# Retention and mixture of experts in one kernel: first expert half tiles beside the gate of the last batch

## The chip, the cores and the metric

One core of one Trainium2 chip. The metric is device time in microseconds of one launch. Before the change the median of three runs is 260.36 us (260.19 to 264.4).

## The reference

Two layers, one after the other. The first is a retention recurrence with a decay per head, over 4 batches, 8 heads, 768 steps and 64 columns. The second sends each of the 3072 rows of its output, 512 wide, through at most one of 8 experts.

```python
# q, k, v: (4, 8, 768, 64) float32
gamma = 1 - 2.0 ** (-5 - arange(H))
for t in range(S):
    state = gamma * state + einsum('bhd,bhe->bhde', k[:, :, t], v[:, :, t])
    y[:, :, t] = einsum('bhd,bhde->bhe', q[:, :, t], state) / sqrt(D)
x = y.transpose(0, 2, 1, 3).reshape(B * S, H * D)          # (3072, 512)

active = x @ w_skip > 0                                    # other rows are passed through
e_idx  = argmax(x @ w_gate, axis=1)                        # 8 experts
gate_w = softmax(x @ w_gate)[e_idx]
out = x;  out[row] += gate_w[row] * (relu(x[row] @ w1[e]) @ w2[e])   # active rows, w1: 512x1024, w2: 1024x512
```

Counted from the reference on the drawn inputs, 1510 rows are active, per expert 191, 133, 229, 179, 211, 187, 160 and 220. Of batches 0 to 2 alone these are 157, 98, 164, 126, 164, 132, 114 and 163.

## The kernel before, in words

**Attention units.** The loop at L471 runs over NU = 16 units `i`, a pair of heads of one batch each (batch `i // 4`). A unit scales the rows of later units on POOL (`scale_rows`, L91), turns rows on PE (`rows_t`, L231), computes states (`kv_states`, L243), scores (`scores`, L275, whose mask multiply `ATm` at L295 is on DVE) and values (`values`, L300, copied out as `xT` by DVE at L321 and ACT at L323). `rows_x` (L326) turns the result back into rows `xall` and in the same matmul makes partial logits `Lp`, copied out by ACT at L340 and L341. `store_x` (L343) writes a batch to `out` by a DMA on ACT's queue.

**Gate.** Each batch's gate is a chain of small steps: `gate_a` (logits, largest, active; DVE), `gate_exp` (ACT), `gate_count` (matmuls that count rows before each row; PE), `gate_pos`, `gate_sum`, `gate_b`, `gate_c` (DVE), `one_hots` (six one-hot matrices of a row's position among 256 slots, L433, DVE), `table` (twelve matmuls, L441, that sum row numbers and weights into a table of slots) and `table_add`. `Rsum` carries the counts over from batch to batch. For batches 0 to 2 the steps stand at fixed places in the units that follow the batch (L493 to L530), all six one-hots of a batch at one place. The last batch's steps stand behind the loop (L538 to L545). `slots` (L554) then turns the table into row indices `si` and weights `g` for both halves of the 256 slots.

**Experts.** An expert has a tile of CAP = 256 slots in NST = 2 parts of 128. `gather` (L579) fetches a part's rows from `out` by an indirect DMA on POOL's queue, six buffers for three experts ahead. `x_tr` (L591) casts them to bf16 on DVE (L595), turns them on PE (L599) and copies them on DVE (L600). `layer1` (L602) has 32 matmuls of 256 columns with four ReLU copies on ACT (L613). `layer2` (L616) has 16 matmuls of 512 columns (L620), a multiply-add with the gathered rows on DVE (L625) and a scatter by indirect DMA (L628). In PE's order the next expert's `x_tr` stands between `layer1` and `layer2`. The number of further passes, for an expert with more than 256 rows, is counted at L640 to L654 and loaded into a register of each engine; the loop at L669 runs that often.

**Weights.** The matrices are cast to bf16 by DMAs on POOL's queue: 28 quarter matrices (`load_piece`) in units 3 to 15 by the counts of `EARLY` (L456), each in the last two units behind a tiny POOL multiply that waits for a named tile, and 9 whole matrices (`load_whole`, L202) in the expert stage: two behind the gathers of expert 1, two behind those of expert 2, and two after each of the first experts until none is left. A drain of POOL stands before the first gather (L569), and one after expert 5 (L665). Instructions of an engine run in the order of the code.

Of the kernel before, what the change touches and what calls it, by code (L numbers as in the profile page):

```python
# [18 lines left out]
def kernel(  # L19
# [38 lines left out]
    NGA = 3  # L58
    NPASS = (N + CAP - 1) // CAP - 1
# [4 lines left out]
    poolC = ctx.enter_context(tc.tile_pool(name="constp", bufs=1))  # L64
    poolW = ctx.enter_context(tc.tile_pool(name="wpool", bufs=1))
# [96 lines left out]
    xrows = [poolC.tile([128, DM], FP32, name=f"xrows{t}") for t in range(NGA * NST)]  # L162
# [180 lines left out]
    def store_x(b, g):  # L343
        A_.dma_start(
            out=out[b * S : (b + 1) * S, :].rearrange("(g p r) d -> p g (r d)", p=128, r=R)[:, g, :],
            in_=xall[b][:, g * R : (g + 1) * R, :].rearrange("p r d -> p (r d)"),
        )
# [4 lines left out]
    def gtile(name, shape, dt=FP32):  # L352
        gt[name] = pool.tile(shape, dt, tag=name, bufs=1, name=name)
        return gt[name]
# [25 lines left out]
    def gate_count(b):  # L380
        ha = gt["ha"]
        cp = psum.tile([128, NCH, E], FP32, tag="T", bufs=2, name="cps")
# [24 lines left out]

    def gate_b(b):
# [28 lines left out]
    def table(js, oh, ps, tag, bufs):  # L437
        tp = ps.tile([128, NST, NV * E], FP32, tag=tag, bufs=bufs, name="tabps")
# [8 lines left out]
    def table_add(tp):  # L447
        t = Tsb[:, :].rearrange("p (s n) -> p s n", s=NST)
        V_.tensor_tensor(t, t, tp[:, :, :], ALU.add)

# [16 lines left out]

    for m in range(3):
        rows_t(0, m)
    kv_states(0)  # L470
    for i in range(NU):  # L471
        b, p = divmod(i - 5, NP)
# [7 lines left out]
        if i >= NP and i % NP == 1:  # L480
            store_x(i // NP - 1, G - 1)
        scores(i, 0)
        scale_rows(i + 2, 0, G_)
# [9 lines left out]
        if b >= 0 and p == 1:  # L493
            gate_count(b)
            gate_pos(b)
        if b >= 0 and p == NP - 1:
            table_add(table(batch_js(b), oh, psum, "T", 2))
# [5 lines left out]
        if b >= 0:  # L503

            if p == 0:
                gate_a(b)
            elif p == 1:
                gate_sum(b)
                gate_b(b)
            elif p == 2:  # L510
                gate_c(b)
                oh = one_hots(batch_js(b), pool)
# [5 lines left out]
        rows_x(i - 1, 1)  # L518
        if not late:
# [3 lines left out]
        if i and i % NP == 0:  # L523
            for g in range(G - 1):
                store_x(i // NP - 1, g)
# [3 lines left out]
        if b >= 0 and p == 0:  # L529
            gate_exp(b)  # L530
# [18 lines left out]

    poolX = ctx.enter_context(tc.tile_pool(name="wlate", bufs=1, reuse_waits="tile"))  # L550
    poolE = ctx.enter_context(tc.tile_pool(name="esb", bufs=2, reuse_waits="tile"))
    psE = ctx.enter_context(tc.tile_pool(name="eps", bufs=2, space=bass.MemoryType.PSUM, reuse_waits="tile"))

    def slots():  # L554

        T = Tsb[:, :].rearrange("p (s a e) -> p s a e", s=NST, a=NV)
        sh = [128, NST, E]
        tid = poolE.tile(sh, FP32, tag="tid", bufs=1, name="tid")
        V_.scalar_tensor_tensor(out=tid[:, :, :], in0=T[:, :, 0, :], scalar=256.0, in1=T[:, :, 1, :], op0=ALU.mult, op1=ALU.add)
        emp = poolE.tile(sh, FP32, tag="emp", bufs=1, name="emp")  # L560
        V_.tensor_scalar(emp[:, :, :], T[:, :, 1, :], 0.0, BIG, ALU.is_equal, ALU.mult)
        si = poolE.tile(sh, I32, tag="si", bufs=1, name="si")
        V_.scalar_tensor_tensor(out=si[:, :, :], in0=tid[:, :, :], scalar=-1.0, in1=emp[:, :, :], op0=ALU.add, op1=ALU.add)
        g = poolE.tile(sh, FP32, tag="g", bufs=1, name="g")
        V_.tensor_tensor(g[:, :, :], T[:, :, 2, :], T[:, :, 3, :], ALU.add)  # L565
        V_.tensor_tensor(g[:, :, :], g[:, :, :], T[:, :, 4, :], ALU.add)
        return si, g

    G_.drain()  # L569
    si, g = slots()  # L570
    xg, xgT = {}, {}

    gathers, scatters = [], []

    def free(ins, others):
        for o in others:
            tc.declare_no_dep(ins, o.ins, reason="the slots of a pass name distinct rows, empty ones none")

    def gather(e, si, first=False):  # L579
        for st in range(NST):  # L580
            t = xrows[(e % NGA) * NST + st]
            ga = G_.indirect_dma_start(  # L582
                out=t[:, :], out_offset=None, in_=out[:, :],
                in_offset=bass.IndirectOffsetOnAxis(ap=si[:, st, e : e + 1], axis=0), bounds_check=N - 1, oob_is_err=False,
            )
            xg[e, st] = t
            if first:
                free(ga.ins, scatters)
                gathers.append(ga)

# [119 lines left out]
```

## Time and profile before

| what | value |
|---|---|
| median of 3 runs | 260.36 us (260.19 to 264.4) |
| profiled execution | 261.43 us |
| its span, first to last instruction | 259.4 us |
| mean granted TensorE clock | 0.922 of full |
| busy: PE, DVE, ACT, POOL | 204.2, 120.5, 85.0, 104.8 us |
| DMA moved, mean rate | 48.72 MB, 188 GB/s |

The span is measured inside the execution; the 2.0 us between it and the execution's own time are around it. In a timeline row the bracket at the end names the idle time of the engine before the row and what ended it.

### The profile page before, as it was taken

Reading aid. Unit: us, or ns where it says so; the run is one execution under the profiler, and the core shown is the slowest. Engines: PE = TensorE matmul, PEld = TensorE weight load, DVE = VectorE, ACT = ScalarE, POOL = GpSimd, SP = SyncE. Lnnn points to the kernel's source line nnn. Section 1 sums busy time; section 2 is a strip of 40 time slices with the busy share of each in tenths; the row PEclk is TensorE's granted clock in tenths of the full one; section 3 lists DMA queues with packets and bytes.
Section 4 is the critical chain, followed back from the end, with each engine's and each line's share of the span. In section 5 each row is a group of like instructions: output and inputs, shape, how many; then the busy total and the mean of one; then the engine's idle time right before and its main releaser. Section 6 shows DMA issues by size and latency. Waiting matters only on the chain.

```text
span 259.4 us, 7927 instructions
## 1 busy us (share of the span) xinstructions
PE 204.2 (79%) x3405; PEld 163.9 (63%) x3405; DVE 120.5 (46%) x348; ACT 85.0 (33%) x192; POOL 104.8 (40%) x129
## 2 busy tenths in 40 slices
PE   2999989987897897995999942189837993988960
PEld 1778878876776786884888731177533662467730
DVE  6344445565677575676565658213402331134220
ACT  5244537433442542541445330032130312033110
POOL 1448466552641642642304310844425463143330
PEclk9999999999999997997999996589995998599995
DMA  6999997999688599467575984599999999241110
GB/s 186 300 241 292 283 268 171 270 311 205 173 204 207 195 246 262 132 111 121 165 163 75 145 160 195 121 197 247 215 260 205 268 238 263 89 139 59 40 56 34
DMA packets 48375, 48.72 MB, mean 188 GB/s; under 512 B 3684, under 2 KB 40548, under 8 KB 47184
## 3 DMA queue, kind: packets, MB, share of 16 engines
q0 software_dynamic: 7888, 22.97, 43.2%
q1 hardware_dynamic: 38720, 18.90, 26.5%
q10 hardware_dynamic: 1728, 6.29, 6.3%
q8 instruction: 29, 0.48, 0.7%
q14 instruction: 10, 0.08, 0.1%
HBM read 56.64 MB, written 10.49 MB: 259 GB/s over the span
## 4 chain that ended last, share of the span: by engine, by line
PE 46%; issue 17%; DMA 15%; DVE 10%; POOL 7%; ACT 1%; POOLq 1%; SPq 0%; ACTq 0%; DVEq 0%
PE tps L240 10%; PE tps L335 9%; PE atps L289 9%; DMA w1b<-in_moe_w_dram 8%; PE yps L313 7%; PE kvps L252 5%; DMA out_dram<-yo,si 5%; PE yps L269 5%; DVE oh L433 4%; POOL xrows L582 3%; POOL out_dram L628 3%; DVE ATm L295 2%; DMA xrows<-out_dram,si 1%; DMA kw<-in_k_dram 1%; PE tabps L441 1%
## 5 line engine op out<-in xcount | busy, mean ns | idle before, releaser
L295 DVE TENSOR_TENSOR ATm<-atps,maskc 128x384 f32<-128x384 f32 x64 | 32.8, 553 | 30.3 <-PE atps L289 29.4
L101 POOL TENSOR_TENSOR qs<-qw,tq 128x768 f32<-128x768 f32 x15 | 22.5, 1501 | 54.1 <-issue 46.8
L613 ACT ACTIVATE hT<-hps 128x512 bf16<-128x512 f32 x32 | 19.1, 597 | 72.9 <-PE hps L609 72.6
L241 ACT COPY QKT<-tps 128x512 f32<-128x512 f32 x48 | 28.0, 586 | 44.3 <-PE tps L240 43.5
L289 PE MATMUL atps<-QKT 64*64 64x128 f32 x768 | 36.7, 278 | 5.8 <-issue 5.0
L335 PE MATMUL tps<-IW,xT 128*128 128x137 f32 x192 | 30.6, 298 | 5.7 <-DVE xT L321 4.8
L628 POOL DMA_INDIRECT out_dram<-yo,si x16 | 16.2, 1014 | 46.1 <-DVE yo L625 34.7
L620 PE MATMUL yps<-w2b,hT 128*128 128x512 bf16 x128 | 33.8, 424 | 0.0
L289 PEld LDWEIGHTS atps<-QKT 64*64 64x64 f32 x768 | 28.7, 138 | 5.9 <-issue 4.4
L609 PE MATMUL hps<-xgT,w1b 128*128 128x256 bf16 x256 | 30.7, 279 | 0.5 <-DVE xgT L600 0.5
L609 PEld LDWEIGHTS <-w1b 128*128 128x128 bf16 x256 | 29.4, 145 | 2.6 <-issue 0.7
L335 PEld LDWEIGHTS tps<-IW,xT 128*128 128x128 f32 x192 | 25.9, 199 | 7.9 <-issue 4.0
L313 PE MATMUL yps<-ATm,vn 64*64 64x128 f32 x768 | 26.3, 272 | 2.8 <-issue 2.6
L101 POOL TENSOR_TENSOR ks<-kw,tk 128x768 f32<-128x768 f32 x15 | 22.4, 1495 | 13.5 <-DMA kw<-in_k_dram 10.1
L323 ACT COPY xT<-yps 64x384 f32<-64x384 f32 x32 | 15.2, 474 | 28.5 <-PE yps L313 27.7
L582 POOL DMA_INDIRECT xrows<-out_dram,si x16 | 16.9, 1053 | 18.4 <-DVE g L565 11.6
L625 DVE SCALAR_TENSOR_TENSOR yo<-yps,g,xrows 128x512 f32<-128x512 f32 x16 | 12.0, 751 | 26.3 <-PE yps L620 26.3
L620 PEld LDWEIGHTS <-hT 128*128 128x128 bf16 x128 | 13.6, 108 | 16.8 <-issue 6.3
L313 PEld LDWEIGHTS yps<-ATm,vn 64*64 64x64 f32 x768 | 21.8, 133 | 3.8 <-issue 2.9
L599 PE MATMUL xtp<-identb,xb 128*128 128x128 bf16 x64 | 7.7, 254 | 20.2 <-DVE xb L595 14.3
L240 PE MATMUL tps<-ident,ks 128*128 128x128 f32 x96 | 18.4, 306 | 4.9 <-DVE ks L101 4.9
L269 PE MATMUL yps<-QKT,St 64*64 64x128 f32 x320 | 20.8, 291 | 0.0
(101 smaller groups left out, 232.2 us busy)
## 6 DMA issues: line engine op xcount, KB each, us to landing
vn<-in_v_dram SPq DMA_DIRECT2D x16, 384.0 KB, 5.7
out_dram<-xall ACTq DMA_DIRECT2D x12, 512.0 KB, 4.6
kw<-in_k_dram SPq DMA_DIRECT2D x15, 384.0 KB, 7.0
qw<-in_q_dram SPq DMA_DIRECT2D x15, 384.0 KB, 7.7
w2b<-in_moe_w_dram POOLq DMA_DIRECT2D x5, 1024.0 KB
w1b<-in_moe_w_dram POOLq DMA_DIRECT2D x16, 256.0 KB
w1b<-in_moe_w_dram POOLq DMA_DIRECT2D x4, 1024.0 KB
w2b<-in_moe_w_dram POOLq DMA_DIRECT2D x12, 256.0 KB
```

What stands on the lines that cost most here:

```text
L101: eng.tensor_tensor(o[:, :, h, :], rows[:, :, h, :], sc[:, :, h, :], ALU.mult)
L240: PE.transpose(out=ps[:, j * 128 : (j + 1) * 128], in_=(ks, qs)[w][i][:, s_, :, :].rearrange("p h d -> p (h d)"), identity=ident[:, :])
L241: A_.copy(out=QKT[i][:, 4 * m : 4 * m + 4, :], in_=ps[:, :].rearrange("p (j t) -> p j t", j=4))
L269: PE.matmul(out=Y[i, c][o : o + 64, g, :], lhsT=St[i][t : t + 64, ch - 1, :], rhs=QKT[i][t : t + 64, NCH + R * g : NCH + R * g + R, 64 * c ...
L289: PE.matmul(out=ps[h][cp, j, :], lhsT=QKT[i][hp, a * SPB + j, cp], rhs=QKT[i][hp, NCH + R * g : NCH + R * g + R, cp], start=True, stop=True,)
L295: V_.tensor_tensor(out=ATm[i, a][:, t, :, :], in0=ps[t][:, :, :], in1=maskc[:, a * SPB : (a + 1) * SPB, :, :].rearrange("p s r t -> p s (r ...
L313: PE.matmul(out=Y[i, c][o : o + 64, g, :], lhsT=vn[i][cp, h * G + g, r * D : (r + 1) * D], rhs=ATm[i, a][cp, h, j, :], start=False, stop=l ...
L335: PE.matmul(out=ps[:, j * XW : (j + 1) * XW], lhsT=xT[i][:, a * (NCH // 2) + j, :], rhs=IW[:, p, :], start=True, stop=True, skip_group_che ...
L582: ga = G_.indirect_dma_start(out=t[:, :], out_offset=None, in_=out[:, :], in_offset=bass.IndirectOffsetOnAxis(ap=si[:, st, e : e + 1], axi ...
L609: PE.matmul(out=ps[:, f, :], lhsT=w1b[e][:, db, :].rearrange("p (c a) -> p a c", a=NFB)[:, fb, :], rhs=xgT[e][:, db, :], start=(db == 0), ...
L620: PE.matmul(out=ps[:, :], lhsT=hT[:, fb, st * 128 : (st + 1) * 128], rhs=w2b[e][:, fb, :], start=(fb == 0), stop=(fb == NFB - 1),)
L628: sc = G_.indirect_dma_start(out=out[:, :], out_offset=bass.IndirectOffsetOnAxis(ap=si[:, st, e : e + 1], axis=0), in_=yo[:, :], in_offset ...
```

## The change

Rows of batches 0 to 2 and of the last batch now get slots apart. A new step `gate_fill` raises each expert's count to at least 128 before the last batch is counted, so that its rows get slots from 128 on, and the first part of each tile is final once batch 2's table is added. `slots` works on a range of parts. The work of the experts becomes a list of tasks: the first parts of experts 0, 1 and 2, then their second parts, then experts 3 to 7 whole. `layer1` takes a tile of 128 or 256 columns, with one PSUM tile of 512 columns for four or two blocks.

Batch 2's gate moves forward by about a unit: its count to the end of unit 13, its one-hots to the end of unit 14, its table, the first slots and the filler to the middle of unit 15, and the first parts of experts 0 to 2 are gathered in unit 15. The one-hots of batches 0 and 1 are made in twos at three places over two units, and their table follows a unit later. The last batch's steps are laid among the first two tasks. The first three tiles are cast and moved by ACT. The last batch is stored through SP's queue. Row buffers become eight. Whole matrices, gathers and scatters follow a written plan by task, and POOL's first drain becomes a tiny multiply that waits for the last rows.

```diff
-    NPASS = (N + CAP - 1) // CAP - 1
+    NPASS = (N + 128 + CAP - 1) // CAP - 1
+    FIRST = 3
+    NROW = 8
...
+    def gate_fill(ps, tag, bufs):
+        cn = ps.tile([128, E], FP32, tag=tag, bufs=bufs, name="cnps")
+        PE.matmul(out=cn[:, :], lhsT=onesb[:, :], rhs=Rsum[:, :], start=True, stop=True)
+        fl = gtile("fl", [128, E])
+        V_.tensor_scalar(fl[:, :], cn[:, :], -1.0, 128.0, ALU.mult, ALU.add)
+        V_.tensor_scalar(fl[:, :], fl[:, :], 0.0, ident[:, 0:1], ALU.max, ALU.mult)
+        V_.tensor_tensor(Rsum[:, :], Rsum[:, :], fl[:, :], ALU.add)
...
+    def rows_of(st, first):
+        return (out[0:NOLD, :], NOLD) if first and st == 0 else (out[:, :], N)
...
+    for b in range(B - 1):
+        i, T = NP * b + NP + 1, (psum, "T", 2)
+        at(i, "b", (gate_a, b))
+        at(i, "end", (gate_exp, b))
+        if b < B - 2:
+            at(i + 1, "mid", (gate_count, b, *T), (gate_pos, b))
+            at(i + 1, "b", (gate_sum, b), (gate_b, b))
+            at(i + 2, "b", (gate_c, b), (one_hots_of, b, 2))
+            at(i + 3, "a", (one_hots_of, b, 2))
+            at(i + 3, "b", (one_hots_of, b, 2))
+            at(i + 4, "mid", (table_of, b, *T))
+        else:
+            at(i, "end", (gate_count, b, *T), (gate_pos, b))
+            at(i + 1, "a", (gate_sum, b), (gate_b, b))
+            at(i + 1, "b", (gate_c, b), (one_hots_of, b, NCH))
+            at(i + 2, "mid", (table_of, b, *T), (slots, slice(0, 1), "0"), (gate_fill, *T))
...
+        if i == NU - 1:
+            for e in range(FIRST):
+                gather(e, 0)
...
     values(NU - 1)
-    rows_x(NU - 1, 0)
-    table_add(table(batch_js(B - 2), oh, psum, "T", 2))
-    rows_x(NU - 1, 1)
     b = B - 1
+    for a in range(2):
+        rows_x(NU - 1, a)
     for g in range(G):
-        store_x(b, g)
+        store_x(b, g, nc.sync)
+    G_.tensor_tensor(junk[:, :], xall[b][0:1, NCH - 1, DM - 1 : DM], xall[b][0:1, NCH - 1, DM - 1 : DM], ALU.mult)
     gate_a(b)
...
+    def layer1(e, xgT):
+        n = xgT.shape[2]
...
+        m = 512 // n
+        for f2 in range(NFB // m):
+            ps = psE.tile([128, m, n], FP32, tag="hps", bufs=2, name="hps")
...
+    tasks = [(e, [0]) for e in range(FIRST)] + [(e, rest) for e in range(FIRST) if rest]
+    tasks += [(e, list(range(NST))) for e in range(FIRST, E)]
+    plan = {
+        None: "W", 0: "s0", 1: "gB W s1", 2: "s2 g3 W g4", 3: "s3 W", 4: "s4 g5 W", 5: "s5 W g6", 6: "s6 W g7", 7: "s7 W W",
+    }
...
+    give(None)
+    xgT = x_tr(*tasks[0], A_.copy, A_.copy)
+    gate_exp(b)
+    for k, (e, sts) in enumerate(tasks):
+        hT = layer1(e, xgT)
+        if k == 0:
+            gate_count(b, psE, "cnt", 1)
+            gate_b(b)
+            gate_pos(b)
+            one_hots_of(b, NCH)
+            gate_c(b)
+        if k == 1:
+            table_of(b, psE, "cnt", 1)
+            slots(slice(1, NST), "1")
+            gate_sum(b)
+        if k == FIRST:
+            n_more = passes()
+        if k + 1 < len(tasks):
+            early = k + 1 < FIRST
+            xgT = x_tr(*tasks[k + 1], A_.copy if early else V_.tensor_copy, A_.copy if early else V_.tensor_copy)
+        yos += layer2(e, sts, hT)
+        give(k)
+        if k == len(tasks) - 3:
+            G_.drain()
```

In the plan W is one whole matrix, g3 the gathers of expert 3, gB the gathers of the second parts of experts 0 to 2, and s the scatters of the tasks done so far. `passes` holds the count of L640 to L654 unchanged.

## Rows read from the trace of the kernel before

**Rows 1.** Busy time by stretch: columns are us, PE, PEld, DVE, ACT, POOL, PEclk, DMA share, GB/s

```profile
154.56:168.60 14.04, 3.12 (x28) 2.04 (x29) 8.37 (x42) 0.24 (x1) 5.87 (x7) 0.61 0.54 169
...
168.60:190.60 22.00, 20.21 (x144) 15.26 (x143) 6.08 (x12) 6.57 (x11) 9.12 (x11) 0.94 1.00 220
...
226.50:250.85 24.35, 22.56 (x162) 16.32 (x160) 7.54 (x14) 7.17 (x12) 7.73 (x8) 1.00 0.19 67
```

**Rows 2.** Timeline of the hole: start, us, engine, line, out<-in, count, idle before

```profile
154.37 0.19 ACT L341 COPY Lp<-tps 128x27 f32<-128x27 f32 x1
...
160.91 0.19 PE L643 MATMUL cnt<-Rsum,onesb 128*128 128x8 bf16 x1 [0.68 <-DVE Rsum L406]
...
161.51 1.09 POOL L582 DMA_INDIRECT xrows<-out_dram,si  x1 [11.59 <-DVE g L565]
...
162.17 0.15 DVE L650 CAST npass_i<-npass 128x1 int32<-128x1 f32 x1
...
164.96 0.52 DVE L595 CAST xb<-xrows 128x512 bf16<-128x512 f32 x1 [2.63 <-DMA xrows<-out_dram,si]
...
168.60 4.89 PE L609 MATMUL hps<-xgT,w1b 128*128 128x256 bf16 x32 [0.52 <-DVE xgT L600]
```

**Rows 3.** Timeline, a stall of the expert stage

```profile
180.91 1.05 POOL L582 DMA_INDIRECT xrows<-out_dram,si  x1 [0.30 <-issue]
...
193.56 1.02 POOL L628 DMA_INDIRECT out_dram<-yo,si  x1 [5.07 <-DMA w1b<-in_moe_w_dram]
...
194.80 0.43 DVE L595 CAST xb<-xrows 128x512 bf16<-128x512 f32 x1 [6.96 <-DMA xrows<-out_dram,si]
...
197.16 5.96 PE L620 MATMUL yps<-w2b,hT 128*128 128x512 bf16 x16
```

**Rows 4.** Chain that ended last, one step: start, us, engine, what

```profile
183.87 20.84 DMA w1b<-in_moe_w_dram
```

**Rows 5.** Timeline, end of the expert stage

```profile
235.22 3.69 PE L609 MATMUL hps<-xgT,w1b 128*128 128x256 bf16 x32
...
243.70 3.69 PE L609 MATMUL hps<-xgT,w1b 128*128 128x256 bf16 x32
...
247.23 3.62 PE L620 MATMUL yps<-w2b,hT 128*128 128x512 bf16 x16
```

**Rows 6.** Timeline, one-hots of batch 1

```profile
113.74 1.52 POOL L101 TENSOR_TENSOR qs<-qw,tq 128x768 f32<-128x768 f32 x1 [3.67 <-issue]
...
113.83 4.18 DVE L433 TENSOR_SCALAR oh<-iotab,posT 128x256 bf16<-128x256 bf16 x6
...
120.07 1.74 PE L335 MATMUL tps<-IW,xT 128*128 128x137 f32 x6 [3.08 <-DVE xT L321]
```

**Rows 7.** Instructions of single lines: durations in ns, least, median, most

```profile
L609 PEld LDWEIGHTS <-w1b x256: 141/144/166, 167.8 to 247.0; 128*128 128x128 bf16 x128
...
L599 PE MATMUL xtp<-identb,xb x64: 219/219/314, 166.0 to 240.2; 128*128 128x128 bf16 x64
...
L441 PEld LDWEIGHTS <-oh x48: 95/100/152, 81.8 to 160.0; 128*128 128x128 bf16 x48
```

**Rows 8.** Timeline of PE, short matmuls

```profile
152.17 0.46 PE L441 MATMUL tabps<-rhsT,oh 128*128 128x40 bf16 x12
...
152.99 0.97 PE L335 MATMUL tps<-IW,xT 128*128 128x137 f32 x6 [0.36 <-ACT Lp L341]
...
239.99 0.42 PE L599 MATMUL xtp<-identb,xb 128*128 128x128 bf16 x4 [0.85 <-DVE xb L595]
```

**Rows 9.** Timeline, gate of batch 2 in unit 13

```profile
133.14 0.66 PE L240 MATMUL tps<-ident,qs 128*128 128x128 f32 x4
...
134.63 0.21 DVE L374 TENSOR_TENSOR ha<-hw,act 128x48 bf16<-128x48 f32 x1
```

**Rows 10.** Costliest groups of the page, one row

```profile
L241 ACT COPY QKT<-tps 128x512 f32<-128x512 f32 x48 | 28.0, 586 | 44.3 <-PE tps L240 43.5
```

**Rows 11.** Instructions of the register load on PE

```profile
L651 PEldq TENSOR_LOAD <-npass_i x1: 486/486/486, 165.5 to 165.5; - x1
```

More of the change, by code (lines that the diff above doesn't have):

```diff
@@ L160 @@
     thr_i = poolC.tile([128, NPASS], I32, name="thr_i")
[L162 removed]
+    xrows = [poolC.tile([128, DM], FP32, name=f"xrows{t}") for t in range(NROW)]
     def gate_constants():
@@ L449, in table_add, with slots, free, gather @@
         V_.tensor_tensor(t, t, tp[:, :, :], ALU.add)
+    def slots(sts, tag):
+        T = Tsb[:, :].rearrange("p (s a e) -> p s a e", s=NST, a=NV)[:, sts, :, :]
+        sh = [128, sts.stop - sts.start, E]
+        tid = poolG.tile(sh, FP32, tag="tid" + tag, bufs=1, name="tid")
+        V_.scalar_tensor_tensor(out=tid[:, :, :], in0=T[:, :, 0, :], scalar=256.0, in1=T[:, :, 1, :], op0=ALU.mult, op1=ALU.add)
+        emp = poolG.tile(sh, FP32, tag="emp" + tag, bufs=1, name="emp")
+        V_.tensor_scalar(emp[:, :, :], T[:, :, 1, :], 0.0, BIG, ALU.is_equal, ALU.mult)
+        si = poolG.tile(sh, I32, tag="si" + tag, bufs=1, name="si")
+        V_.scalar_tensor_tensor(out=si[:, :, :], in0=tid[:, :, :], scalar=-1.0, in1=emp[:, :, :], op0=ALU.add, op1=ALU.add)
+        g = poolG.tile(sh, FP32, tag="g" + tag, bufs=1, name="g")
+        V_.tensor_tensor(g[:, :, :], T[:, :, 2, :], T[:, :, 3, :], ALU.add)
+        V_.tensor_tensor(g[:, :, :], g[:, :, :], T[:, :, 4, :], ALU.add)
+        for st in range(sts.start, sts.stop):
+            slot[st] = si[:, st - sts.start, :], g[:, st - sts.start, :]
+    slot, xg, gathers, scatters = {}, {}, [], []
+    NOLD = (B - 1) * S
+    def free(ins, others):
+        for o in others:
+            tc.declare_no_dep(ins, o.ins, reason="the slots of a pass name distinct rows, empty ones none")
+    def rows_of(st, first):
+        return (out[0:NOLD, :], NOLD) if first and st == 0 else (out[:, :], N)
+    def gather(e, st, first=True):
+        t = xrows[len(gathers) % NROW if first else st]
+        src, n = rows_of(st, first)
+        ga = G_.indirect_dma_start(
+            out=t[:, :], out_offset=None, in_=src,
+            in_offset=bass.IndirectOffsetOnAxis(ap=slot[st][0][:, e : e + 1], axis=0), bounds_check=n - 1, oob_is_err=False,
+        )
+        xg[e, st] = t
+        if first:
+            free(ga.ins, scatters)
+            gathers.append(ga)
+    def scatter(e, st, yo, first=True):
+        dst, n = rows_of(st, first)
+        sc = G_.indirect_dma_start(
+            out=dst, out_offset=bass.IndirectOffsetOnAxis(ap=slot[st][0][:, e : e + 1], axis=0),
+            in_=yo[:, :], in_offset=None, bounds_check=n - 1, oob_is_err=False,
+        )
+        if first:
+            free(sc.ins, scatters + gathers)
+            scatters.append(sc)
     def batch_js(b):
@@ L492 @@
                 weights(i, 2)
[L493 to L497, printed above, removed]
+        do(i, "mid")
         for a in range(1, NA):
@@ L569 @@
[L569 to L589, printed above, removed]
@@ L631, in layer2 @@
             )
             if first:
-                free(sc.ins, scatters + gathers)
-                scatters.append(sc)
-    for e in range(NGA):
-        gather(e, si, first=True)
-        load_whole((0, 2, 2)[e], poolX)
-    thr = poolE.tile([128, NPASS], FP32, tag="thr", bufs=1, name="thr")
-    V_.tensor_copy(thr[:, :], thr_i[:, :])
-    cnt = psE.tile([128, E], FP32, tag="cnt", bufs=1, name="cnt")
-    PE.matmul(out=cnt[:, :], lhsT=onesb[:, :], rhs=Rsum[:, :], start=True, stop=True)
-    top = poolE.tile([128, 1], FP32, tag="top", bufs=1, name="top")
@@ new lines, with give @@
+    rest = list(range(1, NST))
+    tasks = [(e, [0]) for e in range(FIRST)] + [(e, rest) for e in range(FIRST) if rest]
[3 more added lines that the diff above has]
+    }
+    yos = []
+    def give(k):
+        for step in plan.get(k, f"s{k}").split():
+            if step == "W":
+                load_whole(1, poolX)
+            elif step == "gB":
+                for e in range(FIRST):
+                    for st in rest:
+                        gather(e, st)
+            elif step[0] == "g":
+                for st in range(NST):
+                    gather(int(step[1:]), st)
+            else:
+                while yos:
+                    scatter(*yos.pop(0))
```

157 lines of the change are left out of this document (69 added, 88 removed).

## The prediction

> **What bounds the kernel now.** I read four views, in this order: busy time by stretch, the timeline of the holes that it shows, the chain that ended last, and the durations of single forms. By stretch [rows 1]: from 154.56 to 168.60 PE is busy 3.12 of 14.04 us, at 0.61 of its clock; from 168.60 to 190.60 the DMA share is 1.00; after 226.50 PE is busy 22.56 of 24.35 us and the DMA engines 0.19. So the expert stage starts with a hole, is then fed by transfers, and only at its end is bound by PE.
>
> The hole [rows 2]: the last logits are copied out at 154.37 + 0.19 = 154.56. Then comes the gate of the last batch as one chain on DVE with two visits to PE, a gather issued at 161.51, its cast at 164.96 (so 3.45 us from issue to use), and the first expert matmul at 168.60. Nothing of this needs PE much, and no expert can start, because all tokens share one table.
>
> The stalls [rows 3, 4]: the gather issued at 180.91 lets its cast start only at 194.80. It sits behind whole weight matrices in POOL's queue. PE has nothing, and when it resumes 16 matmuls of the second layer take 5.96 us, where 3.62 us is the time at full clock [rows 5]. POOL also stops: its scatter at 193.56 waited 5.07 us for a weight matrix, the transfer eight places before it in POOL's order, and by the code's order I find the same distance wherever a POOL transfer waits for another. One matrix issued at 183.87 took 20.84 us [rows 4]; from 193.56 (an earlier one landed) to 204.71 two matrices, two gathers and two scatters went by, so about 5.6 us each, call it 6 with company.
>
> An expert without stalls costs 243.70 - 235.22 = 8.48 us, the last ends at 247.23 + 3.62 = 250.85, and 8.55 us follow to the end of the span at 259.40 [rows 5]. Expert stage: 250.85 - 154.56 = 96.29 us.
>
> **The change, part by part.** I call the end of the last logits copy Z.
>
> *Six half tiles.* Experts 0 to 2 are now worked in halves: three before and three after the last batch's slots. A half tile has 32 first-layer matmuls of 128 columns, 8 second-layer matmuls and 4 transposes. Second layer: 3.62 / 2 = 1.81 us. Transposes: 0.42 us [rows 8]. The 128-column first layer is not in the trace. Upper bound: its 256-column form, 3.69 / 32 = 115 ns [rows 5]. Lower bound: the transposes, also 128 columns, (0.42 - 0.22) / 3 = 64 ns apart [rows 7, 8]. What decides is the weight load, whose source is strided: 144 ns against 100 ns for the contiguous one-hots [rows 7], and those come every 0.46 / 12 = 38 ns with only 40 columns [rows 8]. 38 + 44 = 82 ns is my value. So 2.62 + 0.42 + 1.81 = 4.85 us a half tile, 29.1 us for six, with bounds 25.6 and 35.4. That is 9.7 us per expert where 8.48 was paid: the halves cost 3.6 us in all, and three of them fill the hole.
>
> The trace spaces its 128-column transposes 64 ns apart [rows 8]. The Trainium skill ("TensorE: Matmul & The Clock Gate", section "Back-to-back issue gap") gives about 81 ns for a load and matmul of 128 columns, which speaks against halving a tile: by it six halves take 28.9 us, by the transposes' spacing 25.6 us.
>
> *Start of the first half tile.* Its rows are gathered in the last unit, behind two or three quarter pieces of weights on POOL, and land around Z. Then a cast on ACT, four transposes, a move on ACT: 0.59 + 0.6 + 0.59 us [rows 8, 10], with hand-overs 2.3 us. PE is nearly idle from Z - 0.6 to Z + 2.3, and it was after 3.08 us of idling that the six matmuls at 120.07 took 1.74 us, 0.97 us being the full-clock time of the same six at 152.99 [rows 6, 8]. I add 1.9 us for a slow first layer; bounds 0 and 3.4.
>
> *Waits that come in.* In tasks 0 and 1 ACT casts the next tile only behind its two activations, and PE's transposes stand before its second layer: 1.0 us each, 2.0. The count and the table matmuls of the last batch now stand in PE's order after the first and second task's first layers: 0.5 us each, 1.0; their inputs (DVE, free of casts) are ready. The pass count stands after task 3's first layer: PE waits for its matmul, DVE's chain and a register load, 162.17 + 0.15 - 160.91 = 1.4, plus 0.49 us [rows 2, 11]: 1.9. Behind it on PE wait the transposes of task 4. Transposing a tile of two parts keeps its wait for the second cast, 1.3 us at the first whole expert. With small gaps of 0.5 us these make 6.7 us.
>
> *The second halves' gathers* wait on DVE for the last batch's slots. On PE: task 0's first layer to Z + 6.8 (2.3 + 1.9 + 2.62), the count to 7.3, the wait for ACT, transposes and second layer to 10.5, task 1's first layer to 13.2, the table to 13.7. On DVE positions, one-hots and values after the count take some 3 us, my part of the 6.95 us from Z to the first gather in the hole [rows 2], so the table waits for nothing; adding it and making the indices takes 1 us, Z + 14.7. The first gather is used 3.45 us later, Z + 18.2. PE comes to its transposes at Z + 19.6 (13.7 + 1.0 + 0.42 + 1.81 + 2.62). So it is hidden with 1.4 us to spare; each microsecond beyond costs one. Queued behind them on POOL: one weight matrix, the scatters of tasks 1 and 2 and the gathers of expert 3, none urgent.
>
> *Weights.* One matrix (expert 3, second layer) is issued at Z + 0.5. The next, expert 4's first, stands behind the new gathers at Z + 18.8, later than now, and the others alternate with scatters, the last two after expert 4 (half tiles end at Z + 40.0, two experts more 57.0, its scatters 59.5). At 6 us each eight of them need 48 us from Z + 18.8, and the last lands near Z + 72; PE wants it at Z + 79.4 (40.0 + 4 x 8.48, then 5.5 us of first layer and transposes). Gathers for experts 3 to 7 are issued 10 to 20 us before use with one or two matrices ahead of each, so at up to 12 us they land in time, by 3 to 10 us. If this cover goes, the price is that of rival A.
>
> *Five whole experts*: 4 x 8.48 + 7.15 (the last, from its start to its last matmul, 250.85 - 243.70 [rows 5]) = 41.1 us.
>
> Expert stage: 2.3 + 1.9 + 29.1 + 6.7 + 41.1 = 81.1 us, against 96.3: **15.2 us gained**.
>
> *The loop of attention units.* One-hots in twos: six in a row took DVE 4.18 us at 113.83, the first held until POOL's 1.52 us scaling ended [rows 6]; PE then waited 3.08 us. Two of them would end near 115.5, giving back 2.6 us, and no slow clock after, 1.1 us (the 0.77 us above and part of the next matmuls). For batch 0 I count nothing, PE stood for instruction issue beside it. The other pairs take 0.5 us in DVE's idle time. Gain 3.7 us; bounds 0 and 5. The gate of batch 2 moves forward by about a unit: its count now stands after the transposes that ended at 133.14 + 0.66 = 133.80, while its input is ready at 134.84 [rows 9]: 1.1 us lost, with the next unit's states queued behind it. In the last unit the table, the first slots and the filler put DVE about 1 us behind, of which the table's removal from the end (0.46 us at 152.17 [rows 8]) gives half back: 0.5 us lost. Sum: **2.1 us gained**. Eight clears of row buffers instead of six and the stores on SP's queue, which is empty by then, cost nothing visible; POOL's drain goes and one tiny wait replaces it.
>
> The Trainium skill ("SBUF — State Buffer", section "Who interferes with whom") says that of DVE in its fast modes and GpSimd the second waits out the other's whole instruction. The trace agrees with the first one-hot [rows 6]; what it would mean for pairs is rival C.
>
> Total: 15.2 + 2.1 = 17.3 us off the profiled span of 259.4, so 242.1. The profiled execution took 261.43 us, 1.07 above the median of 260.36; the change taken off the median gives **243.0 us**.
>
> **Rivals.**
> A. *The feed still stalls PE.* For: matrices and gathers share one queue, and eight transfers back still holds POOL. Against: tasks are spread over more time and slack is 3 us or more. Price: the six experts from 168.60 to 235.22 took 66.6 us where six times 8.48 is 50.9 [rows 2, 5]; the 15.7 us between, in five whole experts of six, 13: 256 us, no change that can be told.
> B. *The clock stays low through all six half tiles* (the slower side). For: the hole ran at 0.61 [rows 1], and half tiles leave PE idle a microsecond or two each. Against: after 168.60 the clock rose at once with steady work. Price: 29.1 us doubled, less 1.9: 270 us. It decides from about 22 us of low clock at full load beyond my term.
> C. *Pairs of one-hots meet POOL at each place.* Three places for two batches, four more meetings of 1.5 us: 6 us, 249 us. Against: POOL's two scalings run at a unit's start, the new places lie in its middle and before its end.
> D. *The change doesn't overlap*: the first gathers come after the gate, queued like the one at 180.91. That one took 13.9 us to its use, not 3.45 [rows 2, 3]: first layer 10.4 us later, on a slow clock for longer, 255 us. Against: only quarter pieces are ahead.
> E. *Cheaper halves*: 64 ns and no slow clock: 3.5 + 1.9 us less, 237.6 us.
>
> **How the numbers follow.** A measurement tells about 2%, 5.2 us: faster is below 255.2, slower above 265.6. Forecast 0.60, E 0.13, C 0.08, A 0.10, D 0.05, B 0.04. Faster: 0.60 + 0.13 + 0.08 and a third of A and D, 0.86; same 0.10; slower 0.04. The dear end: 115 ns a matmul (+6.3) and no gain from the one-hots (+3.7), 253; the cheap end is E with 1.5 us more from the loop, 236.
>
> **What would show it.** Right: expert matmuls of 128 columns 2 to 3 us after the last logits; the gate chain under them; a half tile near 4.9 us; no wait of a cast for a gather over 1 us from expert 3 on; DMA share under 1 in places; PE's wait of 3.08 us after the one-hots under 1 us. Wrong: a cast waiting for gathered rows of the second halves, low clock past the first two tasks, POOL waiting for matrices with PE empty behind it, 128-column matmuls over 100 ns.

## The result and the profile after

The changed kernel takes **244.98 us** (243.54 to 245.68, 4 runs) where the kernel before takes 260.27 us (257.76 to 264.40, 4 runs) beside it: ratio 0.9435, 95% interval 0.9351 to 0.952. The forecast was 243.0 us with 236 to 253 as its range. Here and below a median is of all runs of a kernel, while a ratio is of its fast runs alone, so the two can order close kernels differently. The profiled execution has a span of 243.1 us, 16.3 less than before, at 0.960 of the clock. Z, the end of the last logits copy, lies at 152.63 + 0.19 = 152.82 us.

Busy time by stretch of the changed kernel; columns as in [rows 1]:

```profile
155.71:171.71 16.00, 13.88 (x149) 11.02 (x151) 6.83 (x28) 5.86 (x11) 5.79 (x6) 0.91 0.84 200
171.71:190.91 19.20, 14.71 (x135) 10.65 (x137) 6.21 (x16) 3.58 (x6) 10.68 (x12) 0.82 0.99 217
190.91:224.80 33.89, 30.27 (x222) 22.46 (x225) 12.08 (x24) 9.55 (x16) 14.18 (x16) 1.00 1.00 230
...
231.94:243.10 11.16, 0.00 (x0) 0.00 (x0) 0.75 (x1) 0.00 (x0) 3.93 (x4) 0.74 0.21 75
```

The hole of [rows 1], 3.12 us of PE in 14.04, has become 13.88 in 16.00. From 190.91 the whole experts run at full clock, in the stretch shown with PE busy 0.89 of the time, though the DMA share is 1.00 there. Two stretches are weak: the second half tiles, at 0.82 of the clock, and the end, 11.16 us without one matmul.

Timeline of the changed kernel (the one-hots of batch 1, the half tiles, the end):

```profile
112.81 1.53 POOL L103 TENSOR_TENSOR qs<-qw,tq 128x768 f32<-128x768 f32 x1 [4.90 <-issue]
112.90 3.58 DVE L445 TENSOR_SCALAR oh<-iotab,posT 128x256 bf16<-128x256 bf16 x2
114.89 1.51 POOL L103 TENSOR_TENSOR ks<-kw,tk 128x768 f32<-128x768 f32 x1
118.48 0.97 PE L337 MATMUL tps<-IW,xT 128*128 128x137 f32 x6 [2.41 <-DVE xT L323]
...
152.63 0.19 ACT L343 COPY Lp<-tps 128x27 f32<-128x27 f32 x1
155.71 3.40 PE L657 MATMUL hps<-xgT,w1b 128*128 128x128 bf16 x32 [0.67 <-ACT xgT L645]
162.28 2.12 PE L657 MATMUL hps<-xgT,w1b 128*128 128x128 bf16 x32
165.74 1.06 POOL L494 DMA_INDIRECT xrows<-out_dram,si  x1 [1.16 <-DVE g L475]
167.58 2.13 PE L657 MATMUL hps<-xgT,w1b 128*128 128x128 bf16 x32
169.25 0.43 DVE L640 CAST xb<-xrows 128x512 bf16<-128x512 f32 x1 [0.72 <-DMA xrows<-out_dram,si]
169.73 0.41 PE L644 MATMUL xtp<-identb,xb 128*128 128x128 bf16 x4
171.71 2.14 PE L657 MATMUL hps<-xgT,w1b 128*128 128x128 bf16 x32
173.69 0.17 PE L688 MATMUL cnt<-Rsum,onesb 128*128 128x8 bf16 x1
177.39 0.59 PE L644 MATMUL xtp<-identb,xb 128*128 128x128 bf16 x4 [3.53 <-DVE xb L640]
177.76 3.62 PE L669 MATMUL yps<-w2b,hT 128*128 128x512 bf16 x8
181.18 2.75 PE L657 MATMUL hps<-xgT,w1b 128*128 128x128 bf16 x32
185.72 2.14 PE L657 MATMUL hps<-xgT,w1b 128*128 128x128 bf16 x32
190.91 3.69 PE L657 MATMUL hps<-xgT,w1b 128*128 128x256 bf16 x32
...
228.32 3.62 PE L669 MATMUL yps<-w2b,hT 128*128 128x512 bf16 x15
231.98 0.75 DVE L674 SCALAR_TENSOR_TENSOR yo<-yps,g,xrows 128x512 f32<-128x512 f32 x1 [0.97 <-PE yps L669]
232.22 0.98 POOL L505 DMA_INDIRECT out_dram<-yo,si  x1 [13.65 <-issue]
...
236.08 0.99 POOL L505 DMA_INDIRECT out_dram<-yo,si  x1 [0.30 <-issue]
```

The first half tile starts 2.89 us after Z, and the gather that answers to 161.51 in [rows 2] is issued under the second one. PE turns its rows at 169.73 without a wait. The one long wait left is 3.53 us at 177.39, behind the pass count, with a low clock after it (0.50 from 177.39 to 181.18): eight second-layer matmuls in 3.62 us where seven take 1.89 elsewhere. At the end POOL's scatter at 232.22 has stood 13.65 us for "issue": nothing that it waits for by a semaphore. What held it is POOL's own drain.

Instructions by line in the changed kernel (durations in ns: least, median, most):

```profile
L696 DVEq TENSOR_LOAD <-npass_i x1: 1402/1402/1402, 174.8 to 174.8; - x1
...
L749 POOLq DRAIN  x1: 14034/14034/14034, 217.3 to 217.3; - x1
```

### The profile page after: what moved, and what is told of

Its sections match the earlier page's. It is cut to its first block, busy times and chain, and to the rows that moved or that the text cites. A ratio compares the mean times of both kernels' runs of the same rounds, so it can differ in the third digit from the quotient of the medians.

```text
span 243.1 us, 8139 instructions
## 1 busy us (share of the span) xinstructions
PE 197.9 (81%) x3492; PEld 162.6 (67%) x3502; DVE 119.2 (49%) x350; ACT 88.2 (36%) x198; POOL 105.5 (43%) x132
## 4 chain that ended last, share of the span: by engine, by line
PE 46%; issue 18%; DVE 14%; DMA 9%; POOL 5%; ACT 2%; POOLq 1%; another core or an unknown queue 1%; SPq 1%; DVEq 0%; ACTq 0%
PE atps L291 9%; PE tps L337 8%; PE tps L242 8%; DMA xrows<-out_dram,si 8%; PE yps L315 7%; PE yps L271 5%; PE kvps L254 4%; PE hps L657 3%; DVE oh L445 3%; DVE ATm L297 3%; POOL out_dram L505 2%; DVE St L265 2%; DMA qw<-in_q_dram 1%; PE yps L669 1%; DVE ha L376 1%
## 5 line engine op out<-in xcount | busy, mean ns | idle before, releaser
L505 POOL DMA_INDIRECT out_dram<-yo,si x16 | 16.3, 1020 | 43.6 <-DVE yo L674 23.7
L337 PE MATMUL tps<-IW,xT 128*128 128x137 f32 x192 | 29.1, 288 | 7.4 <-DVE xT L323 5.7
L657 PEld LDWEIGHTS <-w1b 128*128 128x128 bf16 x352 | 32.7, 148 | 3.0 <-issue 1.3
L657 PE MATMUL hps<-xgT,w1b 128*128 128x128 bf16 (+1 forms) x352 | 33.1, 257 | 0.7 <-ACT xgT L645 0.7
L337 PEld LDWEIGHTS tps<-IW,xT 128*128 128x128 f32 x192 | 24.5, 190 | 10.0 <-ACT QKT L243 3.4
L669 PE MATMUL yps<-w2b,hT 128*128 128x512 bf16 x118 | 30.3, 396 | 0.5
L669 PEld LDWEIGHTS <-hT 128*128 128x128 bf16 x128 | 12.5, 101 | 13.5 <-issue 1.6
L342 ACT COPY xall<-tps 128x384 f32<-128x384 f32 x32 | 15.3, 478 | 15.5 <-PE tps L337 13.7
## 6 DMA issues: line engine op xcount, KB each, us to landing
w2b<-in_moe_w_dram POOLq DMA_DIRECT2D x5, 1024.0 KB, 12.5
```

What stands on the lines that cost most here:

```text
L337: PE.matmul(out=ps[:, j * XW : (j + 1) * XW], lhsT=xT[i][:, a * (NCH // 2) + j, :], rhs=IW[:, p, :], start=True, stop=True, skip_group_che ...
L505: sc = G_.indirect_dma_start(out=dst, out_offset=bass.IndirectOffsetOnAxis(ap=slot[st][0][:, e : e + 1], axis=0), in_=yo[:, :], in_offset= ...
L657: PE.matmul(out=ps[:, f, :], lhsT=w1b[e][:, db, :].rearrange("p (c a) -> p a c", a=NFB)[:, fb, :], rhs=xgT[:, db, :], start=(db == 0), sto ...
L669: PE.matmul(out=ps[:, :], lhsT=hT[:, fb, k * 128 : (k + 1) * 128], rhs=w2b[e][:, fb, :], start=(fb == 0), stop=(fb == NFB - 1),)
```

## The experiments

Ratios are to the kernel before, run beside on the same chip, with the 95% interval. Of the totals of 2 to 6 only those of 3a, 5 and 6b lie clear of the changed kernel's interval, above it. The loop alone varies: in the seven profiles of kernels with the same loop (the changed kernel, 1, 2, 3a, 3b, 5 and 7a, on several chips) Z lies between 150.2 and 156.6 us. So parts are read from the profiles, from Z on, one execution each.

**1. The gate ahead of the first task.** It takes the overlap away and leaves all else.

```diff
-    for k, (e, sts) in enumerate(tasks):
-        hT = layer1(e, xgT)
-        if k == 0:
-            gate_count(b, psE, "cnt", 1)
...
+    gate_count(b, psE, "cnt", 1)
...
+    for k, (e, sts) in enumerate(tasks):
+        hT = layer1(e, xgT)
```

> The last batch's count, positions, one-hots, table and second slots are put ahead of the first expert tile again; halves, plan and the rest stay. Theory (the half tiles pay by filling the hole): the first expert matmul moves from 2.9 us after the last logits to 8 or 9 us, two waits of 0.5 us for count and table leave the tasks, the clock is low for some 2 us more: 5 to 7 us longer, 250 to 252 us. Rival (the gain is the feed's, by the written plan; the overlap is worth nothing): within 1 us of the changed kernel's 245.0. Either way far below the 260.3 of before.

Measured: 249.83 us (245.99 to 251.80, 4 runs). Timeline of this kernel:

```profile
157.76 3.57 PE L657 MATMUL hps<-xgT,w1b 128*128 128x128 bf16 x32 [0.67 <-ACT xgT L645]
...
231.87 3.62 PE L669 MATMUL yps<-w2b,hT 128*128 128x512 bf16 x15
```

Here Z is 150.59, so the first layer starts at Z + 7.2 and the last matmul ends at Z + 84.9, where the changed kernel has Z + 2.9 and Z + 79.1. Running the tiles beside the gate is worth 5.8 us on the path of these two executions: 4.3 us by the earlier start, and 1.7 us because the first task took 8.29 us here, at a clock of 0.52, and 6.57 us there, at 0.77. The second part is not sure, since experiment 2 has the changed kernel's order there and a clock of 0.50 as well. The total alone does not show the 5 to 7 us: the runs spread from 246.0 to 251.8 us, and there is no ratio for them.

**2. The pass count, loaded late.** The count is computed where it was; the register load moves behind the first layer of the last task but one.

```diff
         if k == FIRST:
-            n_more = passes()
+            npass_i = passes()
+        if k == len(tasks) - 2:
+            n_more = load_passes(npass_i)
```

> The pass count is computed where it was, its register loads are put behind the last but one task's first layer. Theory (the 3.53 us in which PE stood at 173.9 to 177.4, and the low clock after it, are the price of the register loads): the wait falls to under 1 us, eight second-layer matmuls take 1.8 instead of 3.62 us, and the time falls by 4.5 to 6 us, to 239 to 240.5. Rival (the wait was the gathered rows' or the clock falls anyway): 244 to 245.

Measured: 245.28 us, ratio 0.9451 (0.9374 to 0.9529). Timeline of this kernel:

```profile
171.29 2.12 PE L657 MATMUL hps<-xgT,w1b 128*128 128x128 bf16 x32
174.75 0.41 PE L644 MATMUL xtp<-identb,xb 128*128 128x128 bf16 x4 [1.33 <-DVE xb L640]
...
185.83 3.69 PE L657 MATMUL hps<-xgT,w1b 128*128 128x256 bf16 x32
...
224.78 3.63 PE L669 MATMUL yps<-w2b,hT 128*128 128x512 bf16 x15 [1.38 <-DMA w2b<-in_moe_w_dram]
```

From task 3's first layer to expert 3's: 185.83 - 171.29 = 14.54 us, where the changed kernel has 190.91 - 171.71 = 19.20. So the loads and the low clock behind them cost 4.7 us. The wait was expected to fall under 1 us and fell to 1.33. The total hardly moves, against the 4.5 to 6 us expected, and on the path the last matmul ends at Z + 78.2, only 0.9 us earlier than in the changed kernel. The first task took 2.0 us more than there (8.59 against 6.57 us), the whole of it at the low clock, the last layer waits 1.38 us for its weights, and the scatters are held by the drain as before. Busy time of that first task:

```profile
153.25:161.84 8.59, 7.38 (x50) 5.33 (x51) 3.26 (x16) 2.38 (x5) 0.00 (x0) 0.50 1.05 244
```

**3. Two runs on POOL's drain.** Without it (3a), and with one more of it behind the first whole matrix (3b).

```diff
# 3a
         give(k)
-        if k == len(tasks) - 3:
-            G_.drain()
# 3b
     give(None)
+    G_.drain()
```

> POOL's remaining drain is left out. Theory (it held the last four scatters until 232.2, so the last one left 3.4 us late): the last scatter is issued within 0.5 us of the last multiply-add, the stretch from the last expert matmul to the end shrinks from 11.2 to about 8.5 us, the time by 2.6 us to 242.4. Rival (the end of the program waits for something else, or the drain's work is only moved to the end): no change.

> POOL gets one more drain, behind the first whole matrix, where it idles for some 9 us; the later one stays. Theory (a drain's length grows with the transfers since the one before, so the change, which gave up the first drain, made the second 14.0 us long and so held the last four scatters): the second drain falls under 11 us, the last scatter leaves within 0.6 us of the last multiply-add, the stretch from the last expert matmul to the end falls from 11.2 to 8.5 to 9 us. Rival (the second drain only waits for the last matrices to land): it still ends near 231 and the stretch stays over 10.5 us.

Measured: 3a 249.35 us, ratio 0.9608 (0.9525 to 0.9691); 3b 247.88 us, ratio 0.9418 (0.9293 to 0.9543). In 3a the last scatter is issued at 230.07, right behind its multiply-add, and yet 14.5 us follow the last matmul, because the program's own drain at its end now takes 5.71 us (0.38 in the changed kernel). Instructions by line, 3a:

```profile
L785 POOLq DRAIN  x3: 50/103/5706, 237.0 to 243.3; - x3
```

and 3b, with one line of its timeline:

```profile
L727 POOLq DRAIN  x1: 13637/13637/13637, 155.0 to 155.0; - x1
...
L750 POOLq DRAIN  x1: 10869/10869/10869, 223.0 to 223.0; - x1
...
174.94 0.61 PE L644 MATMUL xtp<-identb,xb 128*128 128x128 bf16 x4 [6.05 <-DVE xb L640]
```

In 3b the last drain falls under 11 us and the stretch behind the last matmul to 8.1 us, as was expected, but the extra drain holds the second halves' gathers, so that PE waits 6.05 us at 174.94 and the last matmul ends at Z + 83.1. Part of the short end is that delay itself: the drain was over 3.8 us before the last matmul ended.

Most of the changed kernel's drain is waiting for transfers under way. The last matrix, issued at 211.12, landed 16.3 us later, at 227.4 (DMA issues of that stretch):

```profile
w2b<-in_moe_w_dram POOLq DMA_DIRECT2D x1, 1024.0 KB, 16.3
```

The last packet of POOL's queue ends at 228.3 and the drain at 217.32 + 14.03 = 231.35: 11.0 us of waiting, and 3.0 us of its own. Read in the same way from the packets, the part behind the last one is 1.5 to 1.9 us in the eight drains with 27 to 37 POOL transfers since the drain before (two each in the kernel before, 3b, 6a and 6b), 3.0 to 3.2 us in the eight kernels with 64, and 4.3 us in 7c with 66. In 3a, with 69 and the last packet 4.1 us gone when the drain began, all of its 5.7 us was of its own. So this part goes with the transfers since the drain before, as the theory of 3b has it, but it is the smaller one.

**4. One-hots: in threes without the first place (4a), or all six in one place again (4b).**

```diff
# 4a
-            at(i + 2, "b", (gate_c, b), (one_hots_of, b, 2))
-            at(i + 3, "a", (one_hots_of, b, 2))
-            at(i + 3, "b", (one_hots_of, b, 2))
+            at(i + 2, "b", (gate_c, b))
+            at(i + 3, "a", (one_hots_of, b, 3))
+            at(i + 3, "b", (one_hots_of, b, 3))
# 4b
+            at(i + 2, "b", (gate_c, b), (one_hots_of, b, NCH))
+            at(i + 3, "mid", (table_of, b, *T))
```

> One-hots of batches 0 and 1: none at the first place, three at each of the other two. Theory (at the first place the pair met both of POOL's scalings, 3.58 us for two): the states of units 8 and 12 start 3 us earlier against their unit, PE's wait of 2.41 us at the logits matmuls of unit 12 goes, time 2 to 4 us shorter, 241 to 243. Rival (PE has other waits there, instruction issue above all): under 1 us shorter.

> The one-hots of a batch in one place again, six in a row, all else as changed. Theory (my prediction's term): DVE holds six of them behind POOL's scaling once, some 4.2 us, TensorE waits about 3 us for what stands behind them on DVE, twice in the run, and the time is 1.5 to 3.7 us longer than the changed kernel's beside it. Rival: the first pair meets two scalings of POOL and loses as much (its two took 3.58 us each), so that the twos gain less than 1 us, hidden in the variation of the loop.

Measured: 4a 243.27 us, ratio 0.9288 (0.9196 to 0.9379); 4b 251.24 us, ratio 0.9492 (0.9388 to 0.9596), beside 0.9433 (0.9364 to 0.9502) for the unedited kernel (run 7). The medians of 4b and run 7 are 3.2 us apart, the intervals overlap. Timeline of 4b:

```profile
112.46 4.17 DVE L445 TENSOR_SCALAR oh<-iotab,posT 128x256 bf16<-128x256 bf16 x6
114.44 1.51 POOL L103 TENSOR_TENSOR ks<-kw,tk 128x768 f32<-128x768 f32 x1
118.70 1.11 PE L337 MATMUL tps<-IW,xT 128*128 128x137 f32 x6 [3.08 <-DVE xT L323]
```

Six one-hots take 4.17 us, two of them 3.58 in the first profile: almost all of it is two meetings with POOL's scalings, and the pair meets both (112.81 and 114.89 above). PE's wait falls from 3.08 to 2.41 us only, 0.7 us of gain. But this is one of two outcomes of the same loop. In 3a and 7a the pair took 3.6 us as well; in 1, 2, 3b and 5 it met one scaling, took 1.7 us, and PE waited 0.3 to 0.6 us, so that the twos gave some 2.5 us. Timeline of 2:

```profile
112.17 1.72 DVE L445 TENSOR_SCALAR oh<-iotab,posT 128x256 bf16<-128x256 bf16 x2
115.88 0.97 PE L337 MATMUL tps<-IW,xT 128*128 128x137 f32 x6 [0.54 <-DVE xT L323]
```

What decides between the two is not known. In 4a nothing stands at that place, and PE runs the same six matmuls at 116.44 without a wait. Its ratio is the lower one, but the interval overlaps that of the changed kernel.

**5. All four early matrices behind the second halves' gathers.**

```diff
-        None: "W", 0: "s0", 1: "gB W s1", 2: "s2 g3 W g4", 3: "s3 W", 4: "s4 g5 W", ...
+        None: "W", 0: "s0", 1: "gB W W W W s1", 2: "s2 g3 g4", 3: "s3", 4: "s4 g5", ...
```

> Plan only: four whole matrices stand together before the gathers of expert 3, none at tasks 2 to 4. Theory (what removed the stalls of before is that each gather has at most one or two matrices ahead of it): the rows of expert 3 come behind four matrices, near 195 to 197, where PE wants them at 187; PE stands for 6 to 10 us before expert 3 and runs slowly after it, 252 to 257 us. Rival (the order in the queue matters little, fewer stalls come from more time): under 2 us longer than 245.0.

Measured: 254.57 us, ratio 0.9789 (0.9716 to 0.9862). Timeline of this kernel:

```profile
188.28 1.02 POOL L505 DMA_INDIRECT out_dram<-yo,si  x1 [3.24 <-DMA w1b<-in_moe_w_dram]
194.40 1.00 POOL L505 DMA_INDIRECT out_dram<-yo,si  x1 [5.11 <-DMA out_dram<-yo,si]
196.03 0.61 PE L644 MATMUL xtp<-identb,xb 128*128 128x128 bf16 x4 [8.05 <-DVE xb L640]
```

The stall of [rows 3] is back: with the matrices in one group PE waits 8.05 us for expert 3's rows. What took the stalls away is the matrices' place between the gathers. On the path the last matmul ends at Z + 90.3, 11.2 us later than in the changed kernel. If the two add, this and the 5.8 us of experiment 1 are 17.0 us, nearly all of the 17.2 us by which the expert stage became shorter (96.3 to 79.1 us): the larger part of the change's gain is the order of matrices and gathers, not the filled hole.

**6. Combinations with the early drain.** 6a is 2, 3b and 4a together; in 6b the second matrix also moves to Z.

```diff
# 6b, beyond 6a
-        None: "W", 0: "s0", 1: "gB W s1",
+        None: "W W", 0: "s0", 1: "gB s1",
```

> Split pass count, early drain and one-hots at two places together. If the three add up: 245.0 less 4.7 (count, low clock), 2.5 (drain) and 2 (one-hots), plus 1.4 for a last matrix that then comes late: 237 us. Rival (the feed takes over as the bound): PE waits 3 us or more for the last expert's matrices, 239 to 241.

> As the one before, with expert 4's first matrix issued beside the first whole one and not behind the second halves' gathers. Theory (the feed stands idle for some 8 us while the gate of the last batch runs): the wait for the last matrix goes, the second halves' rows come up to 2 us later; 1 to 2 us under the one before. Rival (the later rows cost as much as the earlier matrix gives): within 0.5 us of it.

Measured: 6a 247.92 us, ratio 0.9532 (0.9465 to 0.96); 6b 252.90 us, ratio 0.9681 (0.9607 to 0.9755). Both miss what was expected. The early drain took 14.5 and 17.9 us, and PE waited 6.90 and 8.15 us for the second halves' rows behind it: more than the other edits gave.

**7. The changed kernel once more, and the edits without the early drain.** 7a: unedited. 7b: 2 and 4a. 7c: 7b, with the drain one task later.

```diff
# 7c, beyond 7b
-        if k == len(tasks) - 3:
+        if k == len(tasks) - 2:
             G_.drain()
```

> The changed kernel once more, unedited, as the neighbour of the three runs beside it. Theory: the ratio to the kernel before repeats, 0.9435 within 0.01, with the first expert matmul 2 to 3 us after the last logits and the expert stage near 79 us. Rival: the first result was a lucky one, and the ratio lies above 0.955. It also tells how much the time of the loop varies between two executions of the same program.

> Two edits together: the pass count is made where it was and its register is loaded only behind the first layer of the last task but one; one-hots in threes, none at the first place. Theory: 4.7 us less at the pass count and some 1.5 us less in the loop, of which the feed (a matrix that lands late at the last experts) takes 1 to 2 us back: 240 to 241 us where the changed kernel takes 245. Rival: the landing of the last matrices and the held scatters set the end, and the time is within 1 us of the changed kernel's.

> As the run before it, with POOL's drain moved one task later, behind the scatters of the last task but one. Theory: most of the drain's 14 us was waiting for matrices under way; issued near 224 us, when they have landed, it takes 5 to 7 us and holds only the last two scatters, to some 232.5 us, so the time is 2 to 3 us less than in the run beside it. Rival: the drain's own part is as long wherever it stands, it ends near 238 us, and the time is 2 us more or more.

Measured, with one kernel before beside them (262.82 us, 11 runs): 7a 248.01 us (246.06 to 257.63), ratio 0.9433 (0.9364 to 0.9502); 7b 246.22 us (243.86 to 249.28), 0.9353 (0.9281 to 0.9425); 7c 246.39 us (241.33 to 247.81), 0.9246 (0.9148 to 0.9344). The ratio repeats. By the ratios 7c is the best of all and its interval lies below that of 7a; by the medians it is 1.6 us ahead of 7a and level with 7b. Its ratio rests on two of its six runs, so the 2 to 3 us expected from the later drain are shown by the profile's end and not by the total. Last matmul to end of span is 11.7 us in 7b and 8.7 in 7c, as the drain falls from 15.0 to 6.8 us. Instructions by line, 7c:

```profile
L754 POOLq DRAIN  x1: 6762/6762/6762, 229.6 to 229.6; - x1
```

7b was expected to gain 4 to 5 us and gained about 2 (0.9433 - 0.9353, times 262.8). In its profile none of it is left on the path: the last matmul ends at Z + 81.5, in 7a at Z + 81.0. Tasks 3 and 4, where the pass count stands, take 10.9 us in 7b and 12.5 in 7a, only 1.6 us less, since 7a's loads took 0.5 to 0.9 us and not up to 1.4; and the first task lost 1.4 us at a clock of 0.70, where 7a has 1.00. Both profiles also have a wait that the first one lacked, so it does not tell them apart, but it takes up what the changed kernel had to spare. Timeline, 7a:

```profile
170.73 1.06 POOL L494 DMA_INDIRECT xrows<-out_dram,si  x1 [4.89 <-DMA out_dram<-xall]
174.13 0.50 DVE L640 CAST xb<-xrows 128x512 bf16<-128x512 f32 x1 [4.33 <-DMA xrows<-out_dram,si]
174.69 0.61 PE L644 MATMUL xtp<-identb,xb 128*128 128x128 bf16 x4 [3.71 <-DVE xb L640]
```

and one step of the chain that ended last, 7a:

```profile
156.92 12.99 DMA out_dram<-xall
```

The first gather of the second halves reads rows that the last batch's store must have written. Of three stores of 512 KB on SP's queue the slowest took 13.0 us in 7a, the gather's indices had been ready at 166.72 + 0.17, and PE lost 3.71 us. In the first profile the slowest store took 11.1 us, and the gather never waited for it. The same wait stands in 4a, 4b, 7b and 7c (2.9 to 5.3 us on POOL, 1.7 to 4.1 on PE). What lies beside the stores are weights from POOL's queue, at a DMA share near 1. To issue those weights behind the stores was not tried.

## Why the prediction was right, point by point

| term, us | predicted | profile after |
|---|---|---|
| Z to the first layer | 2.3 | 155.71 - 152.82 = 2.9 |
| slow first layer | 1.9 | 3.40 - 2.13 = 1.3 |
| six half tiles | 29.1 | 6 x (171.71 - 167.58) = 24.8 |
| ACT's casts, count and table, task 0 and 1 | 3.0 | 2.3 |
| pass count, with the low clock after it | 1.9 | 5.8 |
| second cast, gaps | 1.8 | 1.1 |
| five whole experts | 41.1 | 231.94 - 190.91 = 41.0 |
| expert stage | 81.1 | 79.1 |
| last matmul to end of span | 8.55 | 11.2 |
| Z, against before | -2.1 | 152.82 - 154.56 = -1.7 |

The measured terms of the half tiles are differences of first-layer starts in the timeline, less 4.13 us for a half tile without waits and less the slow first layer. On the profiled span the forecast was 1.0 us low (242.1 against 243.1): the stage 2.0 too long, the end 2.6 and the loop 0.4 too short. Inside the stage two misses of about 4 us cancel, and that the total came so close is luck. The mechanism was right: the overlap (experiment 1) and the order of the transfers (experiment 5) make up the gain, as far as one execution of each can tell.

*Half tiles: the term was too large.* A 128-column matmul took 2.12 / 32 = 66 ns, not 82: next to the lower bound from the transposes [rows 8], as in rival E. The argument by the weight load failed. In the profile's costliest groups a load takes 148 ns (144 in [rows 7]), but loads overlap, and the matmuls still start 66 ns apart. The Trainium skill ("TensorE: Matmul & The Clock Gate", "Back-to-back issue gap") gives about 81 ns; here the measurement differs, and decides.

*Pass count: too small, and the step is "a register load, 0.49 us".* Two loads stand one behind the other on the path: DVE's next cast stands behind DVE's load, and PE's transposes behind that cast and PE's own load. Here the loads took 1.24 to 1.40 us on four engines and 0.49 on PE, where before all took 467 to 541 ns. DVE's load, before and in experiment 5:

```profile
L651 DVEq TENSOR_LOAD <-npass_i x1: 541/541/541, 162.4 to 162.4; - x1
...
L696 DVEq TENSOR_LOAD <-npass_i x1: 544/544/544, 175.7 to 175.7; - x1
```

The DMA share alone does not make a load long: it was near 0 at the first of these two and near 1 at the second, as it is at the 1402 ns of the changed kernel. PE idled 3.53 us, and the clock then fell to its lower level (0.50), which the sum left out. Experiment 2 gives the whole price, 4.7 us.

*The end, "8.55 us follow": too small.* The sum took the end over from before and put the drains at nothing ("POOL's drain goes and one tiny wait replaces it"). Before, they were these:

```profile
L569 POOLq DRAIN  x1: 7323/7323/7323, 149.3 to 149.3; - x1
...
L665 POOLq DRAIN  x1: 4410/4410/4410, 236.2 to 236.2; - x1
```

The later one was over at 240.6, before the next scatter was ready. Now the only drain took 14.0 us, and four scatters went late, the last at 236.08 instead of right behind 231.98 + 0.75. Of the 9.6 us that it grew by, some 1.2 are of its own (3.0 against 1.9), which can be put down to the drain that went. The rest is waiting: before, the last matrix was issued 27 us ahead of this drain (209.22), and now the last two are issued 6 us ahead of it. 7c, with the same drain one task later, ends 8.7 us after the last matmul.

*The loop: right sum, not shown as a gain.* The twos were to give 3.7 us, 2.6 of them at PE's wait. In the first profile they gave 0.7 us there, since the pair met POOL's second scaling; that is rival C, at the first place only. In four of the seven profiles with this loop they gave about 2.5. The Trainium skill ("SBUF — State Buffer", "Who interferes with whom") had the mechanism, and the trace agrees with it: a one-hot that met a scaling of 1.5 us took 1.5 us or more, where one alone takes about 0.25. The 1.7 us by which Z came earlier are less than Z varies by between executions.

*Gathers hidden with 1.4 us to spare: hidden, with nothing to spare.* In the first profile the cast of these rows ended at 169.68, and PE, done with its first layer at 169.71, turned them without a wait. In 7a the stores, which I had counted at nothing, cost 3.7 us. The three stores of the last batch took 2.7 to 4.4 us before and 5.1 to 11.1 in the first profile after. That is rival D, in part.

*Weights: right, but with less to spare.* The last matrix landed at Z + 74.6, not Z + 72, and PE wanted it at 228.32, Z + 75.5. The prediction's own need, Z + 79.4, was 1.9 us too late by its own stage: 40.0 + 4 x 8.48 + 3.5 = 77.5. Rival A did not come about. Experiment 5 shows its price, 11.2 us on the path where the prediction had 13, and an edit that shortens the stage by more than this 1 us is likely to meet this bound, as in experiment 2. Rival B: in the first profile the low clock lasted for one first layer and for one stretch behind the pass count, no longer; in 1 and 2 it lasted for nearly the whole first task (0.52 and 0.50).

## What to carry to other kernels

A drain costs by what is under way when it begins: after moving transfers later, look up what each drain or wait that stays will meet, and place it behind their landing. When a stage is shortened, look up each transfer whose landing was hidden by the old length (weights, stores that a later gather reads, register loads) and write down its spare time. A forecast whose total is right should still be taken apart term by term: two of mine were off by 4 us in opposite directions.

## What was not expected of the hardware

- POOL's drain lasts until the transfers that POOL issued have landed, and then 1.5 to 4.3 us more, longer with more transfers since the drain before: 14.0 us with two matrices under way and 64 transfers, 6.8 when issued 12 us later, 5.7 at the end of a program that had none before, with nothing under way. What the part behind the landing consists of stays open.
- A register load from SBUF took 0.47 to 0.55 us or up to 1.44 us, both at a DMA share near 1 (0.54 on DVE in 5, 1.40 in the changed kernel). What makes the long ones stays open.
- After 3.5 us without matmuls the clock fell in the changed kernel (second layer 3.62 us, granted clock 0.50) and not in 3a (1.89 us, granted clock 1.00): the idle time alone does not decide. Timeline of 3a:

```profile
177.20 1.89 PE L669 MATMUL yps<-w2b,hT 128*128 128x512 bf16 x8
```

- In 3b, 4b, 5, 6 and 7 the last copy of `xT` on ACT stood 2.9 us for something that the profile only calls remote; in the first profile and in 1, 2, 3a and 4a the same gap was 1.33 us. The experiments of one chip agree; the cause stays open.
